# Work lists searched anew, a limit on loads in flight, padded value rows and one last copy in an attention and softplus MLP kernel

## The chip, the core and the metric

The kernel runs on 1 core of one Trainium2 chip. The metric is device microseconds per execution; three executions of the kernel before took 473.81, 474.37 and 475.50 us, so its time is 474.37 us, the median.

## The reference

Four batches of eight heads, 576 positions, head size 64. Attention is taken twice and added: once on means over 4 neighbouring positions (144 by 144 scores, its result repeated 4 times), once on a band of 7 positions around each position. The sum goes, as 2304 tokens by 512, through two weight matrices with a softplus between them.

```python
q_d = q.reshape(B, H, Sd, factor, D).mean(axis=3)      # k_d, v_d likewise, factor 4
out_d = sm_attn(q_d, k_d, v_d)
out_up = np.repeat(out_d, factor, axis=2)
mask = np.abs(pos[:, None] - pos[None, :]) < factor
attn = softmax(where(mask, scale * q @ k.T, -1e9))
x = out_up + attn @ v                                  # to 2304 x 512
h = x @ w_in                                           # 512 x 2048
g = np.maximum(h, 0.0) + np.log1p(np.exp(-np.abs(h)))
return g @ w_out                                       # 2048 x 512
```

## The kernel before

The eight heads of a batch are four pairs, so there are 16 pairs, numbered 0 to 15; pairs 0 to 3 are batch 0. A pair loads four things through SyncE's queue (SP): `q` and `k` (128x584 each, 292 KB), `vr` (the value rows that are averaged, 72 partitions of 4 KB, 288 KB) and `vw` (the windows of values for the band, 384 KB). VectorE reduces q and k to sums of four (`qd`, `kd`, line 487), `block` lays qd out per head (line 456), TensorE makes the pooled scores (`psd`, line 519) and the banded scores (`psc`, line 580). Then come maximum (`mxd`, `mx`), subtraction (`sub`, line 613), exponential, sum, reciprocal and product, transposes (`sT` on VectorE, `pt0` and `pt1` on TensorE with the copies `sdT0` and `sdT1`), the products with the values (`po`, lines 703 and 726), and `x` (line 757), the pair's 128 columns of the MLP's input. The pooled value rows `vd` are made on GpSimd (lines 504, 507).

`xh` and `xl` split x into two parts that add up to it, and each of the 32 weight tiles (512 KB; `iload`, `oload` with the steps `itop`, `ior`, `ihi`, `ilo`) is unpacked and split the same way, so each product of the MLP is three matmuls. The tokens are cut into groups of 512 (five, the last of 256); for each of 16 hidden tiles the first layer is 12 matmuls (line 896, `l1`), the softplus runs on ScalarE, VectorE and GpSimd, and the second layer is 12 matmuls (line 962, `l2`) that run two tiles behind. In group 0 the first layer's tiles 0 to 2 are cut into 4 pieces, one for each pair: `l1_2.0` is the piece of pair 2 in tile 0.

A planner in Python, `Plan.order`, sets the order in which the instructions are written, engine by engine, and so the order of each engine's queue. It keeps a clock of its own from the costs that stand beside each operation. For the first part of the program it doesn't choose: the lists `ORDER` (line 91) say for each engine which operation comes next (`psd.3` is psd of pair 3, `+4` is four filler matmuls on TensorE, line 1052). Where a list ends, the planner takes the ready operation of the lowest priority number.

Listed loads are spaced by two rules. A load is written when the planner's DMA clock is at most `PACE` ahead (line 302), and it gets a wait on the last load that the planner thinks has landed by then (line 321):

```python
o.behind = next((x for x in reversed(loads) if x.end <= t), None)
```

The second layer's results are copied out of PSUM in four chunks of 128 rows for each group; the last chunk of the last group is copied in halves by VectorE and ScalarE, and each half has its own DMA (line 990).

Of the kernel before, what the change touches and what calls it, by code (L numbers as in the profile page):

```python
# [39 lines left out]
HD = SD // 2  # L40
NR = 3
# [56 lines left out]
        qd.0 kd.0 mx.0 sub.0 qd.2 sum.0 sm.0 kd.1 qd.1 mx.2 kd.2 sT.0 ior.0 mxd.0 mx.1 sub.2 mxd.1
        smd.0 qd.3 sub.1 qd.4 oor.0 smd.1 mxd.2 mask.4 sum.2 ior.1 sm.2 sum.1 kd.4 kd.3 sm.1 smd.2
        mx.4 mx.3 sT.1 sub.3 mxd.3 sdT1.1 ior.2 sub.4 sdT0.1 smd.3 od.0 mxd.4 sum.3 x.0 sm.3 sT.2  # L100
        sdT0.2 sdT1.2 x.1 sT.3 ior.3 oor.1 sdT1.3 od.2 smd.4 x.2 ior.4 xl.1 od.3 x.3 ilo.3 xl.3
# [4 lines left out]
        block.0 exp.0 block.1 expd.0 expd.1 exp.1 normd.0 exp.2 itop.1 block.3 ohi.0 sdT0.0 ihi.1
        expd.2 sdT1.0 normd.2 itop.2 exp.3 block.4 ihi.0 expd.3 normd.3 expd.4 xh.0 od.1 itop.3
        otop.1 sdT0.3 ihi.2 xh.1 itop.4 normd.4 xh.2 ihi.3 ihi.4 exp.4 xh.3 ohi.1 itop.5 fill_xh.0
        abs.0 expln.0 abs.2 expln.2 ihi.5 itop.6 abs.1 expln.1 otop.2 ihi.6 sdT1.4 itop.7 abs.3
# [3 lines left out]
        vd.1 norm.0 itop.0 block.2 vd.0 otop.0 normd.1 olo.0 ilo.1 norm.1 vd.2 norm.2 ilo.0 vd.3
        norm.3 xl.0 ilo.2 xl.2 olo.1 ilo.4 gh.0 ilo.5 gh.2 gh.1 otop.3 olo.3
    """,
    "SP": """
        q.0 k.0 q.2 vr.1 q.1 k.2 k.1 iload.0 vr.0 k.4 q.3 q.4 oload.0 iload.1 k.3 iload.2 vw.0 vr.2
        oload.1 vw.1 vr.3 iload.3 vw.2 iload.4 vw.3 k.5 iload.5 iload.6 q.5 vw.4 oload.2 iload.7
# [983 lines left out]
```

## Time and profile before

| | |
|---|---|
| three executions, median | 474.37 us (473.81 to 475.50) |
| profiled execution, its own time | 476.92 us |
| its span, first to last instruction | 475.0 us |
| mean granted TensorE clock | 0.989 |
| TensorE (PE) busy | 460.2 us, 97% |
| VectorE, ScalarE, GpSimd busy | 278.9, 257.0, 99.1 us |
| DMA moved | 42.87 MB, mean 90 GB/s |

The profile is of one execution. The profiled execution's own time is 1.92 us above its span, which is what lies before the first and after the last instruction. A row of the timeline gives start, duration, engine, source line and shapes, and in brackets how long the engine had been idle and who released it; "issue" is a wait for nothing that the profile shows. A record's end on TensorE is modelled, and records of one engine overlap a little, so distances between starts say more than durations. Two records of TensorE (a weight load and a matmul) stand for each step, and an f32 step is done in two passes.

### The profile page before, as it was taken

To read this page: it belongs to the slowest core of one execution; us is meant where nothing else is said; L and a number is where in the kernel's file an instruction comes from. 1 tells how busy PE (TensorE), PEld (TensorE's weight loads), DVE (VectorE), ACT (ScalarE), POOL (GpSimd) and SP (SyncE) were. 2 spreads that over 40 slices of the span, in tenths; PEclk is the share of its full clock that TensorE was granted. 3 is DMA by queue.
4 is the path that set the end of the run, shared out by engine and by line. 5 is a ranking of instruction groups with operands and counts; after the bars stand their busy time and mean duration, and the time that the engine had idled before them with its cause. 6 is when DMAs were issued, how large, how long until landed. Compare 5 with 4: busy or idle time off the path is not lost.

```text
span 475.0 us, 12565 instructions
## 1 busy us (share of the span) xinstructions
PE 460.2 (97%) x5338; PEld 399.2 (84%) x5338; DVE 278.9 (59%) x556; ACT 257.0 (54%) x560; POOL 99.1 (21%) x147
## 2 busy tenths in 40 slices
PE   5799999999999999999999999999999999999996
PEld 3577888888878888888888888888888888889996
DVE  5877888988899666666276647463332222223322
...
GB/s 234 292 227 140 222 158 259 168 210 164 265 100 95 156 2 111 1 110 11 50 52 148 52 61 52 35 1 1 2 88 2 0 2 0 0 1 90 0 1 46
DMA packets 15944, 42.87 MB, mean 90 GB/s; under 512 B 1809, under 2 KB 2449, under 8 KB 15889
## 3 DMA queue, kind: packets, MB, share of 16 engines
...
q8 instruction: 42, 0.69, 0.6%
q14 instruction: 14, 0.11, 0.1%
q10 hardware_dynamic: 144, 0.07, 0.0%
...
## 4 chain that ended last, share of the span: by engine, by line
PE 85%; DMA 6%; DVE 5%; issue 2%; ACT 1%; POOLq 0%; SPq 0%; DVEq 0%; ACTq 0%
PE acc L962 36%; PE h L896 36%; PE psc L580 3%; PE po L726 2%; PE psd L519 2%; PE po L703 2%; PE po L714 2%; DMA qT<-in_qt_dram 2%; DMA kT<-in_kt_dram 2%; PE pdt L678 1%; DMA stage<-in_vrow_dram 1%; DMA wro<-in_w_out_dram 1%; DVE t L926 1%; DVE gl L943 1%; DVE qd L487 1%
## 5 line engine op out<-in xcount | busy, mean ns | idle before, releaser
L935 POOL TENSOR_SCALAR gh<-t 128x512 fp32r<-128x512 f32 (+1 forms) x80 | 53.6, 670 | 292.2 <-DVE t L926 210.1
L917 ACT ACTIVATE t<-h 128x512 f32<-128x512 f32 (+1 forms) x80 | 44.2, 552 | 126.6 <-PE h L896 119.4
L926 DVE SCALAR_TENSOR_TENSOR t<-h,t 128x512 f32<-128x512 f32 (+1 forms) x80 | 50.8, 635 | 92.4 <-ACT t L921 74.7
L943 DVE TENSOR_TENSOR gl<-t,gh 128x512 fp32r<-128x512 f32 (+1 forms) x80 | 52.1, 651 | 42.4 <-POOL gh L935 42.2
L896 PE MATMUL h<-xh,wi0h 128*128 128x512 f32 (+1 forms) x160 | 58.8, 367 | 0.6 <-DVE t L926 0.6
L962 PE MATMUL acc<-gh,wo0h 128*128 128x512 f32 (+1 forms) x160 | 58.3, 364 | 0.0
L896 PE MATMUL h<-xh,wi1h 128*128 128x512 f32 (+1 forms) x160 | 58.0, 362 | 0.2 <-DVE t L926 0.2
L962 PE MATMUL acc<-gh,wo1h 128*128 128x512 f32 (+1 forms) x160 | 57.9, 362 | 0.0
L896 PE MATMUL h<-xl,wi1h 128*128 128x512 f32 (+1 forms) x160 | 57.3, 358 | 0.2 <-issue 0.2
L962 PE MATMUL acc<-gl,wo1h 128*128 128x512 f32 (+1 forms) x160 | 57.4, 359 | 0.1
L896 PE MATMUL h<-xl,wi0h 128*128 128x512 f32 (+1 forms) x160 | 57.3, 358 | 0.0
L896 PE MATMUL h<-xh,wi0l 128*128 128x512 f32 (+1 forms) x160 | 57.3, 358 | 0.0
L962 PE MATMUL acc<-gl,wo0h 128*128 128x512 f32 (+1 forms) x160 | 57.3, 358 | 0.0
L962 PE MATMUL acc<-gh,wo0l 128*128 128x512 f32 (+1 forms) x160 | 57.3, 358 | 0.0
L896 PE MATMUL h<-xh,wi1l 128*128 128x512 f32 (+1 forms) x160 | 57.3, 358 | 0.0
L962 PE MATMUL acc<-gh,wo1l 128*128 128x512 f32 (+1 forms) x160 | 57.3, 358 | 0.0
L920 ACT ACTIVATE t<-t 128x512 f32<-128x512 f32 (+1 forms) x80 | 47.1, 589 | 2.3
L921 ACT ACTIVATE t<-t 128x512 f32<-128x512 f32 (+1 forms) x80 | 47.0, 587 | 2.5
L896 PEld LDWEIGHTS h<-xh,wi0h 128*128 128x128 f32 x160 | 30.3, 189 | 4.4 <-DVE t L926 0.8
L896 PEld LDWEIGHTS h<-xh,wi1h 128*128 128x128 f32 x160 | 30.3, 190 | 4.0 <-DVE t L926 0.6
L896 PEld LDWEIGHTS h<-xh,wi1l 128*128 128x128 f32 x160 | 30.3, 190 | 3.8 <-issue 0.4
L962 PEld LDWEIGHTS acc<-gl,wo1h 128*128 128x128 f32 x160 | 30.3, 190 | 3.5 <-DVE gl L943 0.3
(100 smaller groups left out, 781.3 us busy)
## 6 DMA issues: line engine op xcount, KB each, us to landing
...
```

Of the source, the lines that this page charges most:

```text
L519: nc.tensor.matmul(pd3()[:, r, :], qb[:, r * RD : (r + 1) * RD], kd.t, start=True, stop=True)
L580: nc.tensor.matmul(pc()[o : o + HW, t, :], q.t[hp, c : c + HW], k.t[hp, c : c + HW], start=not early or t == 0, stop=not early, skip_group ...
L703: nc.tensor.matmul(pd()[j * D : (j + 1) * D, :], v[:, c, j, :], sdT.t[:, c, j, :], start=(c == 0 and i == 0), stop=(c == 1 and i == len(vs ...
L714: nc.tensor.matmul(po[i].t[o : o + HW, k * QT : (k + 1) * QT].rearrange("p (h w) -> p h w", h=2), vw.t[kp, t, m * HW : (m + 1) * HW], wide ...
L896: nc.tensor.matmul(turned(h.t, n), w[:, cc, fs], turns(x.t[:, cc], g), start=(cc == 0 and k == 0), stop=(cc == NCC - 1 and k == 2),)
L917: op("ACT", c, pr, lambda: nc.scalar.activation(out=tv(), in_=hh(), func=AF.Abs), r=[h], w=[tt], name=("abs", i))
L920: nc.scalar.activation(out=tv(), in_=tv(), func=AF.Exp, scale=-1.0)
L921: nc.scalar.activation(out=tv(), in_=tv(), func=AF.Ln, bias=1.0)
L926: lambda: nc.vector.scalar_tensor_tensor(out=tv(), in0=hh(), scalar=0.0, in1=tv(), op0=ALU.max, op1=ALU.add),
L935: lambda: nc.gpsimd.tensor_scalar(out=gh.t[:, :, cols(g)], in0=tv(), scalar1=1.0, scalar2=0.0, op0=ALU.mult, op1=ALU.add),
L943: lambda: eng[ge].tensor_tensor(out=gl.t[:, :, cols(g)], in0=tv(), in1=gh.t[:, :, cols(g)].bitcast(F32), op=ALU.subtract),
L962: nc.tensor.matmul(turned(acc[g][m].t, n), w[:, f % FB, ms], turns(a.t, g), start=(f == 0 and k == 0), stop=(f == NF - 1 and k == 2),)
```

## The change

The lists are new ones. The planner's DMA model now moves data at 0.27 instead of 0.305 KB per ns, and spaces listed loads by size: a load waits for that earlier load behind which at most 1000 KB are under way, and the planner adds 0.6 us to its landing. `vr` has 80 partitions instead of 72 (8 rows of padding that the host adds and nothing reads), in all 16 pairs. The last chunk of the last group is one copy of 256 columns by VectorE and one DMA on ScalarE's queue. Costs of two operations that no listed kernel path uses (`sums`, and `po` with `V_PE`, which is empty) change without effect. Fillers in the lists go from 16 to 19.

```diff
+VROWS = 80
 ORDER = {
     "PE": """
-        psc.0 psd.0 psc.2 +1 psc.1 psd.1 psc.4 psd.2 +2 pt0.0 +4 pt1.0 psc.3 pt1.1 +2 psd.3 po.0
+        psc.1 psc.0 psc.4 psd.0 psd.1 +6 psc.2 +3 pt1.0 psd.2 psc.3 +1 pt0.0 +2 psd.4 +2 po.0 pt1.2
...
     "SP": """
-        q.0 k.0 q.2 vr.1 q.1 k.2 k.1 iload.0 vr.0 k.4 q.3 q.4 oload.0 iload.1 k.3 iload.2 vw.0 vr.2
+        q.1 k.1 q.0 k.0 k.4 vr.0 q.4 iload.0 q.2 iload.1 k.2 oload.0 k.3 q.3 vr.2 iload.2 vw.0 vr.3
...
-    DMA_RATE = 0.305
-    PACE = 2.2
+    DMA_RATE = 0.27
+    PACE_KB = 1000
+    SIGNAL = 0.6
...
+    def ahead(self, loads):
+        kb = 0
+        for x in reversed(loads):
+            kb += x.kb
+            if kb > self.PACE_KB:
+                return x
+        return None
...
-                    if fixed and o.kb and dma_free + self.DMA_LAT - self.PACE > t + 1e-9:
-                        continue
+                    if fixed and o.kb:
+                        o.behind = self.ahead(loads)
+                        if o.behind and o.behind.end + self.SIGNAL > t + 1e-9:
+                            continue
...
-                        o.behind = next((x for x in reversed(loads) if x.end <= t), None)
                         loads.append(o)
...
-        vr = abuf(u, "stage", [HD, 2, 2, FACTOR, D], 4, 3)
-        load(vr, vrow[u], u - 56 if early else s + 4, 288, ("vr", u))
+        vr = abuf(u, "stage", [VROWS, 2, 2, FACTOR, D], 4, 3)
+        load(vr, vrow[u], u - 56 if early else s + 4, 300, ("vr", u))
...
-                for e, q, k in (("DVE", "SP", 0), ("ACT", "ACT", 1)):
-                    o = buf("stage", [P, 2, GN], 4, f"osb{g}_{m}{k}")
-                    cs = slice(k * n // 2, (k + 1) * n // 2)
-                    emit(e, q, m, o, lambda o=o: o.t[:, 0, : n // 2], cs)
+                o = buf("stage", [P, 2, GN], 4, f"osb{g}_{m}")
+                emit("DVE", "ACT", m, o, lambda o=o, m=m: o.t[:, 0, :n], slice(0, n))
                 continue
...
+    vrow = _np.pad(vrow.reshape(NU, HD, -1), ((0, 0), (0, VROWS - HD), (0, 0)))
```

What the new lists move is seen in three places. In the rows, the number right after a name is the pair's (`qT0`, `kT1`; `stage1` is `vr` of pair 1, `wri0` is `iload.0`); the number behind it is a buffer's.

SyncE's queue at the start of the program, before:

```order
L427 DMA qT0_138<-in_qt_dram 128x584
L427 DMA kT0_140<-in_kt_dram 128x584
L427 DMA qT2_142<-in_qt_dram 128x584
L427 DMA stage1_144<-in_vrow_dram 72x1024
L427 DMA qT1_148<-in_qt_dram 128x584
L427 DMA kT2_204<-in_kt_dram 128x584
L427 DMA kT1_210<-in_kt_dram 128x584
L828 DMA wri0_219<-in_w_in_dram 128x2047
L427 DMA stage0_278<-in_vrow_dram 72x1024
```

and now:

```order
L437 DMA qT1_138<-in_qt_dram 128x584
L437 DMA kT1_140<-in_kt_dram 128x584
L437 DMA qT0_142<-in_qt_dram 128x584
L437 DMA kT0_144<-in_kt_dram 128x584
L437 DMA kT4_146<-in_kt_dram 128x584
L437 DMA stage0_200<-in_vrow_dram 80x1024
L437 DMA qT4_206<-in_qt_dram 128x584
L838 DMA wri0_262<-in_w_in_dram 128x2047
L437 DMA qT2_276<-in_qt_dram 128x584
```

Two whole pairs (1 and 0) now come first, with pair 4 behind them; pairs 0, 2 and 1 were mixed before, so that the second pair's k was the sixth load and is now the fourth.

VectorE's queue up to the subtraction of pair 3's banded scores (`sc3<-psc3`; `wro0` is the unpacking of a weight tile), before:

```order
L625 TENSOR_REDUCE smp1_70<-sc1_443 128x12
L487 TENSOR_REDUCE kd4_547<-kT4_285 128x144
L487 TENSOR_REDUCE kd3_556<-kT3_434 128x144
L546 TENSOR_REDUCE sm1_559<-smp1_70 128x12
L547 RECIPROCAL sm1_559<-sm1_559 128x12
L546 TENSOR_REDUCE smd2_566<-smdp0_69 96x3
L547 RECIPROCAL smd2_566<-smd2_566 96x3
L608 TENSOR_REDUCE mx4_575<-sc4_476 128x12
L608 TENSOR_REDUCE mx3_584<-psc3_497 128x12
L665 STREAM_TRANSPOSE sT1_589<-sc1_443 128x384
L613 TENSOR_TENSOR sc3_648<-psc3_497,mx3_584 128x384
```

and now:

```order
L618 TENSOR_REDUCE mx2_469<-psc2_384 128x12
L497 TENSOR_REDUCE qd3_477<-qT3_436 128x144
L675 STREAM_TRANSPOSE sT0_490<-sc0_280 128x384
L623 TENSOR_TENSOR sc2_545<-psc2_384,mx2_469 128x384
L540 TENSOR_REDUCE mxd2_549<-psd2_479 96x3
L635 TENSOR_REDUCE smp0_68<-sc2_545 128x12
L618 TENSOR_REDUCE mx3_568<-psc3_492 128x12
L623 TENSOR_TENSOR sc3_573<-psc3_492,mx3_568 128x384
L556 TENSOR_REDUCE sm2_575<-smp0_68 128x12
L557 RECIPROCAL sm2_575<-sm2_575 128x12
L556 TENSOR_REDUCE smd2_583<-smdp0_69 96x3
```

The same work stands ahead of that subtraction except `sm.2`, `smd.2` (two short rows each) and the unpacking `oor.0` (`wro0`), which now stand behind it; it is the 34th listed operation and was the 37th.

The end of ScalarE's queue, before:

```order
L921 ACTIVATE t4_15_5834<-t4_15_5834 128x2x128
L979 COPY osb4_0_5867<-acc4_0_5393 128x256
L979 COPY osb4_2_5870<-acc4_2_5401 128x256
L979 COPY osb4_31_5876<-acc4_3_5405 128x128
L985 DMA out_0_dram<-osb4_31_5876 128x128
```

and now:

```order
L930 ACTIVATE t4_15_5840<-t4_15_5840 128x2x128
L931 ACTIVATE t4_15_5840<-t4_15_5840 128x2x128
L989 COPY osb4_0_5873<-acc4_0_5399 128x256
L989 COPY osb4_2_5876<-acc4_2_5407 128x256
L995 DMA out_0_dram<-osb4_3_5878 128x256
```

ScalarE's half copy of the last chunk is gone, and the DMA that it issues carries the whole chunk.

## Rows read from the trace of the kernel before

**Rows 1.** The page: TensorE's records, and the DMA queue that fetches TensorE's instructions.
```profile
PE 460.2 (97%) x5338; PEld 399.2 (84%) x5338; DVE 278.9 (59%) x556; ACT 257.0 (54%) x560; POOL 99.1 (21%) x147
...
q8 instruction: 42, 0.69, 0.6%
```

**Rows 2.** Windows: busy us and records of five engines, granted clock, DMA share, GB/s.
```profile
24.86:28.27 3.41, 3.17 (x13) 2.45 (x15) 2.44 (x8) 2.61 (x8) 3.33 (x5) 0.50 0.60 190
...
39.49:58.38 18.89, 18.89 (x198) 16.34 (x199) 14.43 (x27) 16.09 (x29) 8.35 (x8) 1.00 0.53 180
58.38:150.00 91.62, 90.61 (x1174) 77.70 (x1173) 80.65 (x146) 71.63 (x151) 22.12 (x22) 1.00 0.55 179
150.00:469.88 319.88, 319.80 (x3102) 282.60 (x3100) 153.81 (x314) 146.02 (x312) 41.84 (x71) 1.00 0.12 40
```

**Rows 3.** Timeline of TensorE, 0 to 60 us.
```profile
9.81 1.01 PE L580 MATMUL psc<-kT,qT 64*32 64x32 f32 x96 [3.33 <-DMA kT<-in_kt_dram]
...
13.66 1.38 PE L580 MATMUL psc<-kT,qT 64*32 64x32 f32 x82 [1.98 <-issue]
...
25.56 1.06 PE L1052 MATMUL busy<-identb 128*128 128x512 bf16 x2
...
27.99 0.83 PE L703 MATMUL po<-sdT,vd 72*64 72x144 f32 x8
...
31.29 1.24 PE L1052 MATMUL busy<-identb 128*128 128x512 bf16 x5
...
39.49 0.43 PE L726 MATMUL po<-sT,vw 32*64 32x24 f32 x16 [0.96 <-issue]
...
58.38 0.38 PE L962 MATMUL acc<-gh,wo0h 128*128 128x512 f32 x1
```

**Rows 4.** Timeline of VectorE, 0 to 45 us.
```profile
3.65 0.75 DVE L487 TENSOR_REDUCE qd<-qT 128x144 f32<-128x576 f32 x1 [2.08 <-DMA qT<-in_qt_dram]
4.35 0.75 DVE L487 TENSOR_REDUCE kd<-kT 128x144 f32<-128x576 f32 x1
...
10.45 0.75 DVE L487 TENSOR_REDUCE kd<-kT 128x144 f32<-128x576 f32 x1 [1.83 <-DMA kT<-in_kt_dram]
...
15.51 0.56 DVE L608 TENSOR_REDUCE mx<-psc 128x12 f32<-128x384 f32 x1 [0.80 <-PE psc L589]
...
19.51 0.68 DVE L850 SCALAR_TENSOR_TENSOR wro<-wro,top 128x512 int32<-128x512 int32 x1
...
22.60 0.23 DVE L547 RECIPROCAL sm<-sm 128x12 f32<-128x12 f32 x1
...
26.82 0.56 DVE L613 TENSOR_TENSOR sc<-psc,mx 128x384 f32<-128x384 f32 x1
```

**Rows 5.** Windows of 10 us, columns as in rows 2.
```profile
0.00:10.00 10.00, 4.95 (x132) 2.73 (x136) 4.89 (x11) 2.45 (x4) 5.90 (x28) 1.00 0.75 218
10.00:20.00 10.00, 7.82 (x305) 6.28 (x293) 8.30 (x16) 4.00 (x17) 5.78 (x8) 0.66 0.93 297
```

**Rows 6.** Timeline of GpSimd, 0 to 45 us.
```profile
8.54 1.26 POOL L504 TENSOR_TENSOR stage<-stage 72x512 f32<-72x512 f32 x1 [2.64 <-DMA stage<-in_vrow_dram]
9.88 0.72 POOL L507 TENSOR_TENSOR vd<-stage 72x256 f32<-72x256 f32 x1
...
13.36 1.02 POOL L458 TENSOR_SCALAR block<-qd 64x144 f32<-64x144 f32 x2
```

**Rows 7.** The chain that ended last, 78 to 88 us.
```profile
78.17 3.65 DMA qT<-in_qt_dram
...
84.32 3.24 DMA stage<-in_vrow_dram
```

**Rows 8.** Timeline of TensorE, 76 to 150 us.
```profile
89.38 0.48 PE L896 MATMUL h<-xh,wi1h 128*128 128x512 f32 x1 [0.16 <-DVE t L926]
```

**Rows 9.** Timeline of all engines, 469.5 to 475 us.
```profile
470.75 0.42 DVE L981 COPY osb<-acc 128x256 f32<-128x256 f32 x1 [0.92 <-PE acc L962]
...
471.74 0.27 ACT L979 COPY osb<-acc 128x128 f32<-128x128 f32 x1 [0.29 <-DVE osb L981]
```

More of the change, by code (lines that the diff above doesn't have):

```diff
@@ L96 @@
+        l1_1.1 l1_2.0 l1_1.2 l1_3.0 l1_2.1 l1_3.1 l1_2.2 pt0.4 l1_3.2 l1_0.3 l1_0.4 l2.0 l2.1
     """,
     "DVE": """
[L98 to L101, printed above, removed]
@@ L102 @@
-        sum.4 ior.5 max.0 sm.4 fill_xl.0 gl.0 max.2 ior.6 max.1 gl.2 qd.5 gl.1 ilo.6 oor.2 norm.4
-        max.3 oor.3 olo.2 sT.4 kd.5 oor.4
+        kd.1 qd.1 qd.0 mx.1 sub.1 kd.4 sum.1 mx.0 sm.1 kd.0 sub.0 qd.4 sum.0 ior.0 qd.2 mask.4 mxd.0
+        mx.4 mxd.1 sT.1 sm.0 smd.0 ior.1 kd.2 smd.1 kd.3 mx.2 qd.3 sT.0 sub.2 mxd.2 sum.2 mx.3 sub.3
+        sm.2 smd.2 ior.2 mxd.4 sub.4 sum.3 oor.0 norm.2 x.0 sT.2 mxd.3 sm.3 norm.3 xl.0 smd.4 sT.3
+        od.2 smd.3 x.2 ior.3 vd.3 od.1 x.1 oor.1 xl.1 sum.4 x.3 ior.4 xl.3 ilo.4 olo.1 ior.5 sm.4
@@ L104 @@
+        max.0 oor.2 max.1 gl.0 ilo.5 norm.4 olo.2 max.2 gl.1 sdT0.4 ior.6 fill_xl.0 oor.3 max.3
+        oor.4
     """,
     "ACT": """
[L106 to L109, printed above, removed]
@@ L110 @@
-        expln.3 abs.4 ohi.2 expln.4 ohi.3 otop.4 sdT0.4 block.5
+        exp.1 exp.0 itop.0 block.1 ihi.0 itop.1 expd.0 expd.1 ihi.1 normd.0 otop.0 sdT1.0 normd.1
+        exp.2 block.4 expd.2 exp.3 sdT0.0 block.3 normd.2 expd.4 od.0 sdT1.2 ohi.0 exp.4 sdT0.2 xh.0
+        ihi.2 itop.3 expd.3 sdT1.1 sdT0.1 normd.3 normd.4 xh.2 sdT1.3 sdT0.3 otop.1 xh.1 sdT1.4
+        ihi.3 od.3 itop.4 xh.3 ohi.1 ihi.4 itop.5 abs.0 expln.0 abs.1 expln.1 ihi.5 ohi.2 abs.2
+        expln.2 otop.3 itop.6 fill_xh.0 abs.3 expln.3 otop.4 itop.7 ohi.3
@@ L111 @@
     """,
     "POOL": """
[L113 to L114 removed]
+        vd.0 block.0 norm.1 block.2 ilo.0 ilo.1 norm.0 vd.2 itop.2 vd.1 ilo.2 olo.0 xl.2 ilo.3
+        otop.2 gh.0 gh.1
     """,
     "SP": """
[L117 to L118 removed]
@@ L342, in order @@
             nxt += [port] if port > t else []
-            nxt += [x.end for x in loads if x.end > t]
-            nxt += [dma_free + self.DMA_LAT - self.PACE] if dma_free + self.DMA_LAT - self.PACE > t else []
+            nxt += [x.end + self.SIGNAL for x in loads if x.end + self.SIGNAL > t]
             for pend in waiting.values():
@@ L504, in pool_v @@
             e.tensor_tensor(
-                out=vr.t[:, :, :, 0:2], in0=vr.t[:, :, :, 0:2], in1=vr.t[:, :, :, 2:4], op=ALU.add
+                out=vr.t[:HD, :, :, 0:2], in0=vr.t[:HD, :, :, 0:2], in1=vr.t[:HD, :, :, 2:4], op=ALU.add
             )
-            e.tensor_tensor(out=vd.t, in0=vr.t[:, :, :, 0], in1=vr.t[:, :, :, 1], op=ALU.add)
+            e.tensor_tensor(out=vd.t, in0=vr.t[:HD, :, :, 0], in1=vr.t[:HD, :, :, 1], op=ALU.add)
         if not v_pe:
@@ L698, in mm_pv @@
         def mm_pv():
-            vs = [vr.t[:, :, :, f] for f in range(FACTOR)] if v_pe else [vd.t]
+            vs = [vr.t[:HD, :, :, f] for f in range(FACTOR)] if v_pe else [vd.t]
             for c in range(2):
@@ L732, in mm_pv @@
                         )
-        op("PE", 1.85 if pair else 2.2, sV + 0.5, mm_pv, r=[vr if v_pe else vd, (sdT, 0), (sdT, 1), vw] + (wide_keys if pair else [sT]), w=po, lat=gap, block=not early, name="po")
+        op("PE", 1.85 if pair else 4.5 if v_pe else 2.2, sV + 0.5, mm_pv, r=[vr if v_pe else vd, (sdT, 0), (sdT, 1), vw] + (wide_keys if pair else [sT]), w=po, lat=gap, block=not early, name="po")
         od = abuf(u, "od", [P, SD], 1, 2)
```

10 lines of the change are left out of this document (5 added, 5 removed).

## The prediction

> **What bounds the kernel now.** I read the windows first, cut where TensorE changes its work. From 58.38 us, where the second layer's second tile begins, to 150 us TensorE is busy 90.61 of 91.62 us, and from there to 469.88 us 319.80 of 319.88 [rows 2]. Behind 58.38 us there is thus 1.1 us to gain, and what the change can move lies ahead of it or in the last 5 us. The timeline of TensorE splits what lies ahead [rows 3]. From 27.99 us, the first `po`, to 58.38 us it goes on without a wait but one, 0.96 us in the middle of a `po`, that is put down to "issue". Ahead of 27.99 us it waits for loads (3.33 us at 9.81), for nothing visible (1.98 us at 13.66), and in one stretch it runs at a granted clock of 0.50, the 1.2 GHz level [rows 2]: two fillers take 1.06 us there, and five take 1.24 us at 2.4 GHz [rows 3]. So two numbers make the time: when the first `po` starts, and what TensorE executes from there to the common point M, at which batch 0's four `po`, pair 4's transposes, five tiles of the first layer and one of the second are done (58.38 us).
>
> **When the first po starts.** In the new list, `psd.4` and two fillers stand ahead of `po.0`. `psd.4` takes one of the two PSUM banks, which comes free when VectorE has subtracted pair 3's banded scores (`sub.3`). So VectorE's queue sets this start. That subtraction ended at 26.82 + 0.56 = 27.38 us [rows 4], 23.7 us after VectorE's first reduction at 3.65. In those it waited 1.83 us for the k that was the sixth load and 0.80 us for scores that TensorE's stall held back; other waits were under 0.7 us. The new list takes three entries out of the way: `oor.0`, 0.68 us, and `sm.2` and `smd.2`, four short rows that I price at 0.23 each [rows 4], together 1.6 us. The work itself is then 23.7 - 1.83 - 0.80 - 1.6 = 19.5 us. It now begins with `kd.1` and so at the second load, which VectorE got at 4.35 us or earlier [rows 4]; that gives 23.85 us with no wait of these two kinds. Do they come back? The order of loads gives VectorE two whole pairs at once, and the waits on pair 2's mix are gone. What is late next is k of pair 4, the fifth load, and q of pair 4, the seventh; I add 0.4 us for them: 24.3 us. Two fillers and a `psd` took from 25.56 to 27.99, 2.4 us, at the lower clock [rows 3], so about 1.2 at the higher: `po.0` starts between 25.5 and 26.7 us. From below it is bounded by its own load: `vw.0` is the 17th load in both lists with 6.1 MB up to its end; 5.15 MB had moved by 20 us, and at 297 GB/s [rows 5] the rest takes 3.2 us, at the mean of 258 GB/s 3.7, after which it still has to land: 24 to 25 us. From above: if the waits of 1.83 and 0.80 us come back, it is 28.0 us, as before. I take 26.0 us, nearer the lower end, because VectorE's own work leads there, and keep 25.0 and 28.0.
>
> Off this path on TensorE: `psc.4` is now the third `psc`, as `psc.1` was when TensorE stalled for 1.98 us [rows 3]; nothing needs its scores before `mask.4`, the 16th entry of VectorE's list, so a stall there costs nothing up to some 3 us. Were that cover gone, the stall would go to `psd.0` and on to VectorE. On GpSimd `block.0` now stands behind `vd.0`, and so behind the sixth load. That load was served at 9.81 us [rows 3]; 1.26 + 0.72 + 1.02 us [rows 6] put `psd.0` at 12.8 us. `mxd.0` is the 17th entry of VectorE's list, some 10 us behind 4.35, so 1.5 us are left; with a stage load that lands 2 us late VectorE would stand for 0.5 us. I count nothing.
>
> **From po.0 to M.** 58.38 - 27.99 = 30.39 us, less the issue wait of 0.96, is 29.4 us [rows 3]. The new list has five fillers there instead of seven, -0.5 us at 0.25 each, and three transposes more, which I price between nothing and those fillers, 0.4 us: 29.3 us. The issue wait may come again or not; I count half, 0.5 us. M is then at 26.0 + 29.3 + 0.5 = 55.8 us: 2.6 us earlier, with 25.0 + 29.3 = 54.3 (-4.1) and 28.0 + 30.3 = 58.3 (-0.1) as ends. The Trainium skill, "Runtime: NRT & Kernel Launch", section "Instruction fetch mechanics", says that instructions come in blocks of 256 by a DMA of the engine's own and that this is mostly hidden. Rows agree with the size, 42 packets of 0.69 MB for 10,676 records, 254 each [rows 1]; not with the hiding, if the waits of 1.98 and 0.96 us are fetches. By that rule the half wait falls away and the sum would be 0.5 us better.
>
> **Behind M.** TensorE's work is the same; 1.1 us of waits remain as they are. A start 2.6 us earlier meets softplus and weights on VectorE and ScalarE earlier. At 89.38 us TensorE already waits 0.16 us for VectorE [rows 8], so there is no reserve in that spot. But the chain that leads there starts at TensorE itself: q of pair 6 is loaded when TensorE has freed its buffer at 78.17 us [rows 7], so most of it moves along. I add 0.3 us, between 0 and 2.6.
>
> **The padding.** 16 loads carry 32 KB more, four of them early: 0.13 MB, at most 0.4 us of DMA time at 297 GB/s [rows 5], inside the 24 to 25 us above. A lone 72-row load took 3.24 us, a q load next to it 3.65 [rows 7]; nothing there shows that 72 rows are slow. The Trainium skill, "DMA: Bandwidth & Descriptors", section "Why a DMA increments its semaphore by 16 and not by 1", has a load run on the largest number of engines up to 16 that divides its rows: 12 for 72, 16 for 80, so five rows for each engine instead of six. By it a lone load would be up to 0.5 us shorter (estimate, a sixth of 3.24); the sum stays, since no `vr` ends last on the path above.
>
> **The end.** ScalarE's half copy waited 0.29 us for VectorE's half and ended at 472.01 us. VectorE now copies 256 columns from the same start, 471.45, in 0.42 us [rows 9], so the last DMA goes out at 471.9 us instead of 472.0, and SyncE has one issue less. It carries 128 KB instead of 64. -0.2 us, between -0.4 and +0.2.
>
> **Sum.** -2.6 + 0.3 - 0.2 = -2.5 us. The profiled execution took 476.92 us, 2.55 above the median; 474.4 there is 471.9 us as a run.
>
> **Rivals.**
> 1. *The other engines hold the second layer.* If VectorE and ScalarE don't come forward with TensorE, what was gained at M is waited for between 58 and 110 us. For it: no reserve at 89.38 us [rows 8]. Against: VectorE is busy 80.65 of 91.62 us [rows 2], and the chain starts at TensorE. Time: 474.4 - 0.2 = 474.2 us, no change.
> 2. *The start isn't earlier.* The new rule lets 1000 KB be under way, but the queue was mostly full before: DMA share 0.93 in 10 to 20 us [rows 5]. If loads set `po.0` and land as before, only the end and the padding remain: 474.2 us. Against: the first `po` wasn't held by its load but by TensorE's and VectorE's queues.
> 3. *Instructions come late.* More loads under way share the DMA engines with the fetch of TensorE's instructions. A `po` uses some 208 records in 2.3 us; one of the four stalled 0.96 us, and a denser stretch earlier 1.98 [rows 3]. If all four stall by 1.5 us, the mean of those two, M comes 6.0 - 0.5 = 5.5 us later than forecast: 477.4 us, slower. It is slower by over 0.3% from 1.1 us per `po` on. Against: the share was near its limit already. The same page of the Trainium skill speaks against it, since it has the fetch hidden.
>
> **How the numbers follow.** Of this kernel 0.3%, 1.4 us, can be told from no change. Forecast: 0.60, with a range of its own of 470.1 to 473.6; 0.56 of it is faster by over 1.4 us, 0.04 not. Rival 1: 0.15, of which 0.04 slower (waits that exceed what was gained). Rival 2: 0.11, of which 0.02 slower. Rival 3: 0.14, of which 0.12 slower. Together faster 0.56, same 0.26, slower 0.18. The range runs from 469.9 (both lower ends of the sum, -4.1 and -0.4) to 475.3, which takes in rivals 1 and 2 and leaves out most of rival 3.
>
> **What would show it.** Right: `po.0` at 25 to 27 us, `sub.3` ending ahead of 25 us, the second tile of the second layer at 54.5 to 57 us, no new wait of TensorE over 1 us between there and 110 us, the last output DMA going out 0.1 us after the copy. Wrong: a first `po` at 28 us or later (rival 2); waits of TensorE for VectorE or ScalarE that grow behind 58 us (rival 1); issue waits within the `po` groups that sum to over 4 us (rival 3).

## The result, and the profile after

The changed kernel takes **481.42 us** (median of 4 executions, 480.44 to 481.92), the kernel before 474.94 (473.81 to 475.54, 4). The ratio is 1.0137 with a 95% interval of 1.0109 to 1.0165: slower by 1.4%, where 471.9 us was forecast. The profiled execution took 481.25 us with a span of 479.5, against 476.92 and 475.0 of before. By the profiles it is thus 4.3 us slower, by the medians 6.5, since the profiled execution of before lay 2 us above its median.

TensorE first: its timeline, with the first `po`, the first tile of the first layer (`l1_0.0`), the third `po`, and the common point M.

```profile
25.85 0.71 PE L713 MATMUL po<-sdT,vd 72*64 72x144 f32 x8
26.49 1.59 PE L736 MATMUL po<-sT,vw 32*64 32x24 f32 x96
...
33.41 0.57 PE L906 MATMUL h<-xh,wi0h 128*128 128x512 f32 x1
35.31 0.80 PE L906 MATMUL h<-xl,wi0h 128*128 128x512 f32 x1 [1.33 <-DVE xl L789]
...
36.46 1.23 PE L713 MATMUL po<-sdT,vd 72*64 72x144 f32 x8
37.62 2.88 PE L736 MATMUL po<-sT,vw 32*64 32x24 f32 x96
...
64.05 0.38 PE L972 MATMUL acc<-gh,wo0h 128*128 128x512 f32 x1
```

The first `po` starts at 25.85 us instead of 27.99 [rows 3], as forecast. M comes at 64.05 instead of 58.38. What lies between has grown from 30.39 to 38.20 us. Two things in these rows do it: a wait of 1.33 us for VectorE's `xl`, and `po` groups that take 1.23 and 2.88 us where the first `po` took 0.71 and 1.59. The windows, the first two cut where the granted clock changes, show the second (columns as in [rows 2]):

```profile
17.32:34.38 17.06, 15.19 (x455) 11.11 (x453) 15.71 (x34) 15.08 (x51) 9.14 (x9) 1.00 0.83 261
34.38:51.45 17.07, 16.14 (x232) 13.10 (x233) 10.52 (x24) 8.78 (x19) 3.78 (x4) 0.50 0.50 163
...
58.38:150.00 91.62, 91.53 (x1180) 78.99 (x1179) 83.14 (x148) 73.81 (x151) 15.57 (x20) 1.00 0.57 184
...
150.00:469.88 319.88, 319.88 (x3085) 282.32 (x3084) 155.47 (x318) 148.21 (x317) 42.23 (x70) 1.00 0.13 41
```

For 17 us TensorE runs at the 1.2 GHz level although it is busy for 16.14 of them. The clock fell 0.4 us after the wait for `xl` had begun, so 0.93 us of the wait lie in that stretch. Before, TensorE had 3.4 us at that level around the start of the first `po`, and from there to M none [rows 2]. Behind 58.38 us TensorE waits 0.09 us instead of 1.1.

Why `xl` was late stands in the timelines of VectorE and GpSimd:

```profile
23.84 0.56 DVE L623 TENSOR_TENSOR sc<-psc,mx 128x384 f32<-128x384 f32 x1
...
31.58 3.67 DVE L789 TENSOR_TENSOR xl<-x,xh 128x512 fp32r<-128x512 f32 x1
```
```profile
29.92 1.28 POOL L514 TENSOR_TENSOR stage<-stage 72x512 f32<-72x512 f32 x1 [4.14 <-DMA stage<-in_vrow_dram]
31.27 0.97 POOL L517 TENSOR_TENSOR vd<-stage 72x256 f32<-72x256 f32 x1
32.21 1.26 POOL L885 TENSOR_TENSOR wi0l<-wri,wi0h 128x512 fp32r<-128x512 f32 x1
33.44 1.27 POOL L885 TENSOR_TENSOR wo0l<-wro,wo0h 128x512 fp32r<-128x512 f32 x1
```

`xl.0` took 3.67 us. The same subtraction takes 0.68 us on VectorE elsewhere in this trace. It started inside a row of GpSimd operations (`vd.1`, `ilo.2`, `olo.0`) that follow one another with no gap, and it ended at 35.25 us, 0.54 behind the row's last. The row began when `vr.1` had landed, 4.14 us after GpSimd had become free. The new list loads `vr.1` as the 20th of its loads (before, as the fourth), and puts `xl.0` on VectorE (before, on GpSimd).

The chain of waits runs through it (start, duration, what):

```profile
31.66 3.60 DVE xl L789
35.26 0.04 issue
35.31 1.22 PE h L906 x2
```

The end, a timeline of all engines:

```profile
475.92 0.42 DVE L991 COPY osb<-acc 128x256 f32<-128x256 f32 x1 [0.24 <-PE acc L972]
476.38 0.37 ACTq L995 DMA_DIRECT2D out_dram<-osb  x1
```

The DMA goes out 0.04 us after VectorE's copy has ended, and the span ends 3.1 us behind that; before, the DMA went out at 472.03 us and the span ended 2.9 behind.

### The profile page after: what moved, and what is told of

Same layout as the page of the kernel before. It is cut to its first block, busy times and chain, and to the rows that moved or that the text cites. A ratio compares the mean times of both kernels' runs of the same rounds, so it can differ in the third digit from the quotient of the medians.

```text
span 479.5 us, 12567 instructions
## 1 busy us (share of the span) xinstructions
PE 467.8 (98%) x5341; PEld 405.3 (85%) x5341; DVE 283.3 (59%) x559; ACT 259.5 (54%) x566; POOL 82.7 (17%) x139
## 4 chain that ended last, share of the span: by engine, by line
PE 92%; DMA 5%; DVE 2%; POOL 1%; issue 0%; POOLq 0%; SPq 0%
PE h L906 40%; PE acc L972 39%; PE po L736 2%; PE psc L590 2%; PE po L713 2%; DMA stage<-in_vrow_dram 2%; PE po L724 2%; PE psd L529 2%; PE pdt L688 2%; DMA wro<-in_w_out_dram 1%; DMA qT<-in_qt_dram 1%; DVE xl L789 1%; DMA kT<-in_kt_dram 1%; POOL stage L514 0%; DVE sc L642 0%; DVE mxd L540 0%
## 5 line engine op out<-in xcount | busy, mean ns | idle before, releaser
L945 POOL TENSOR_SCALAR gh<-t 128x512 fp32r<-128x512 f32 (+1 forms) x80 | 49.2, 615 | 303.0 <-DVE t L936 209.0
L953 DVE TENSOR_TENSOR gl<-t,gh 128x512 fp32r<-128x512 f32 (+1 forms) x80 | 51.3, 641 | 41.6 <-POOL gh L945 41.4
L906 PE MATMUL h<-xh,wi0h 128*128 128x512 f32 (+1 forms) x160 | 60.3, 377 | 0.0
L906 PE MATMUL h<-xl,wi0h 128*128 128x512 f32 (+1 forms) x160 | 58.8, 367 | 1.3 <-DVE xl L789 1.3
L906 PE MATMUL h<-xh,wi0l 128*128 128x512 f32 (+1 forms) x160 | 58.6, 366 | 0.0
L906 PEld LDWEIGHTS h<-xl,wi0h 128*128 128x128 f32 x160 | 31.1, 195 | 5.0 <-DVE xl L789 1.7
L906 PEld LDWEIGHTS h<-xh,wi0l 128*128 128x128 f32 x160 | 31.1, 194 | 3.6
L972 PEld LDWEIGHTS acc<-gh,wo0h 128*128 128x128 f32 x160 | 30.3, 189 | 3.6
```

The source lines that it names most:

```text
L906: nc.tensor.matmul(turned(h.t, n), w[:, cc, fs], turns(x.t[:, cc], g), start=(cc == 0 and k == 0), stop=(cc == NCC - 1 and k == 2),)
L945: lambda: nc.gpsimd.tensor_scalar(out=gh.t[:, :, cols(g)], in0=tv(), scalar1=1.0, scalar2=0.0, op0=ALU.mult, op1=ALU.add),
L953: lambda: eng[ge].tensor_tensor(out=gl.t[:, :, cols(g)], in0=tv(), in1=gh.t[:, :, cols(g)].bitcast(F32), op=ALU.subtract),
L972: nc.tensor.matmul(turned(acc[g][m].t, n), w[:, f % FB, ms], turns(a.t, g), start=(f == 0 and k == 0), stop=(f == NF - 1 and k == 2),)
```

## The experiments

Theory T: GpSimd's row holds up `xl.0`, TensorE stands idle for it, and the clock falls. Its rivals: A, `xl.0` is slow for another reason; B, the clock falls whatever that wait does; C, pacing, padding or the last chunk lose the time; and, from the first runs on, F, the forecast's third rival: instructions come late. Each ratio is to the kernel before in the same comparison. In these comparisons single executions of one edited kernel spread by 0.4 to 2%, those of the kernel before by 2 to 3%, so a ratio's interval is about 0.003 to 0.005 wide on either side. A profile is one draw: those of e2, e6, e8 and e14 are of the slowest execution of their kernel. "Mean clock" is the granted clock, averaged over a kernel's executions.

**First comparison: one piece at a time**

`e1_olo_later`, one entry of GpSimd's list:
```diff
-vd.1 ilo.2 olo.0 xl.2 ilo.3
+vd.1 ilo.2 xl.2 olo.0 ilo.3
```


> The changed kernel with one entry of GpSimd's list moved: olo.0 behind xl.2, so that GpSimd's last operation beside VectorE's xl.0 is ilo.2. Theory T (VectorE's subtraction xl.0 took 3.67 instead of 0.69 us because GpSimd worked back to back beside it; TensorE's wait of 1.33 us that followed brought the 1.2 GHz stretch of 17 us): GpSimd's row ends at about 33.5 instead of 34.7, xl.0 ends near 34.0 instead of 35.25, TensorE's wait is under 0.4 us; if the clock then holds the time is 473 (half clock of 17 us gone, some 6.5 us, and 1.2 us of wait), if it still falls 480. Rival A (xl.0 is slow for a reason that isn't GpSimd, loads for one): xl.0 still takes over 3 us and the time is 481. Rival B (the clock falls whatever this wait does, for what TensorE did earlier): xl.0 is shorter and the half clock comes all the same, 480.

Measured: 1.0085 (1.0050 to 1.0120), mean clock 0.980. The gain didn't come. The timelines of VectorE and GpSimd say why: `vr.1` landed later still, so the shorter row ran at the same time.

```profile
34.22 2.43 DVE L789 TENSOR_TENSOR xl<-x,xh 128x512 fp32r<-128x512 f32 x1
```
```profile
33.96 0.92 POOL L517 TENSOR_TENSOR vd<-stage 72x256 f32<-72x256 f32 x1
34.85 1.26 POOL L885 TENSOR_TENSOR wi0l<-wri,wi0h 128x512 fp32r<-128x512 f32 x1
```
GpSimd's row ends at 36.11 us, `xl.0` at 36.65, again 0.54 behind it. TensorE waited 1.92 us and 13.65 us of half clock followed. So one entry less is no cure while the load is late; the mechanism is the same, which speaks against A.

`e2_fillers`, in TensorE's list:
```diff
-pt0.1 +1 l1_0.0
+pt0.1 +9 l1_0.0
```


> The changed kernel with nine fillers instead of one ahead of the first tile of the first layer, l1_0.0, so that TensorE executes about 8 x 0.215 = 1.7 us of filler matmuls where it otherwise waits. Theory T: xl.0 still takes over 3 us, but TensorE has no idle stretch over 0.7 us between 30 and 36 us, its granted clock stays at 2.4 GHz, and the time is 475 (some 6.5 us better than the changed kernel, 0.3 lost on fillers). Rival B: the half clock comes all the same, 481. Rival A says the same as T here, as it disputes only why xl.0 is slow.

Measured: 0.9991 (0.9954 to 1.0028), mean clock 0.991: the loss is gone within the interval. But in its profile `xl.0` came a moment ahead of GpSimd's operation and took 0.68 us, so the profile doesn't show a filled wait. It shows other stalls: 2.37 us for issue in the middle of `psc.3` and 0.92 us in `po.3`, each with 3.4 us of half clock. The fillers also give late instructions time, 0.22 us for each, so this run alone doesn't tell T from F.

`e3_vr1_early`, in SyncE's list (with e1's edit):
```diff
-vw.0 vr.3 vw.2 vr.1 iload.3
+vw.0 vr.1 vr.3 vw.2 iload.3
```


> The changed kernel with the load of pair 1's value rows, vr.1, ahead of vr.3 and vw.2 instead of behind them, and olo.0 behind xl.2 on GpSimd. Theory T: vr.1 lands two loads (some 2 us) earlier, GpSimd does vd.1 by 29 us instead of 31 and ilo.2 ahead of xl.0; xl.0 takes under 2 us, TensorE waits under 0.4 us for it, the clock stays at 2.4 GHz from 18 us on, M (the second tile of the second layer) is at 55.5 to 57.5 us instead of 64.05, and the time is 472.5, below the kernel before. Rival A: xl.0 still takes over 3 us, 481. Rival B: half clock again, 480.

Measured: 0.9982 (0.9932 to 1.0032); the median of its executions isn't below the kernel before's. `vd.1` was done at 29.77 us. `xl.0` fell beside one GpSimd operation, `ilo.2`, took 1.76 us and ended 0.55 behind it, and nobody waited for it (VectorE, GpSimd):

```profile
34.28 1.76 DVE L789 TENSOR_TENSOR xl<-x,xh 128x512 fp32r<-128x512 f32 x1
```
```profile
34.06 1.43 POOL L885 TENSOR_TENSOR wi0l<-wri,wi0h 128x512 fp32r<-128x512 f32 x1 [4.29 <-ACT wi0h L879]
```
M was at 60.70, not at 55.5 to 57.5, because TensorE waited in its timeline at another place:

```profile
24.22 0.85 PE L590 MATMUL psc<-kT,qT 64*32 64x32 f32 x45 [3.10 <-issue]
```
A part of T holds, and F comes in as a second possible cause.

`e4_old_lists`: the five lists of the kernel before in the changed kernel.
```diff
-(the changed kernel's ORDER)
+(the ORDER of the kernel before)
```


> The changed kernel with the five lists of the kernel before; the pacing rule of 1000 KB, the data rate, the padding and the last chunk's copy stay as changed. Theory T (the whole loss comes of the new lists at one place): 475, within 1 us of the kernel before, with half clock for some 3.4 us from 25 us on as before and none from 35 to 52 us. Rival C (the loss lies in pacing, padding or the last chunk): 479 to 482.

Measured: 1.0013 (0.9974 to 1.0052). Its M is at 58.62 us, as before, with half clock from 38.6 to 42.0 us and none other behind 22 us. Windows, columns as in [rows 2]:

```profile
29.29:38.59 9.30, 9.13 (x271) 7.12 (x272) 7.45 (x19) 7.28 (x23) 9.14 (x9) 1.00 0.86 262
38.59:42.01 3.42, 3.42 (x14) 2.36 (x14) 3.39 (x9) 1.52 (x4) 0.64 (x1) 0.50 0.75 239
```
TensorE had been busy for 9.13 of the 9.30 us ahead of that fall, with no single wait over 0.2 us. So a stretch of half clock can also come without a wait right ahead of it, and what brought this one stays open. Pacing, padding and last chunk with the old lists change nothing that can be told; C falls. The loss comes with the new lists.

**Second comparison: where the wait comes from**

`e5_again` is the changed kernel, with no edit.

> The changed kernel as it is, once more, beside the three that follow and on the same chip: where the data lands at other times, the stall may sit in another place. All theories: ratio to the kernel before 1.010 to 1.016. Theory T, sharpened by the runs so far (VectorE's subtraction of two SBUF tensors, xl.0, waits until GpSimd ends the last of its back-to-back operations, and ends 0.55 us behind it): where xl.0 starts within GpSimd's row of vd.1, ilo.2 and olo.0 it ends 0.50 to 0.60 us behind that row, TensorE waits 1 to 2 us ahead of the first tile of the first layer, and half clock follows within 1.5 us for over 10 us. Rival F (late instructions): what stretches the start is the wait for issue in the middle of psc.3, and half clock follows that one.

Measured: 1.0066 (1.0022 to 1.0111), mean clock 0.978. That is slower again, but by 3 us and not the 6.5 of the first result, and below the 1.010 that was expected. The collision is there again, the same (timelines of VectorE, GpSimd, TensorE):

```profile
32.55 3.68 DVE L789 TENSOR_TENSOR xl<-x,xh 128x512 fp32r<-128x512 f32 x1
```
```profile
34.41 1.27 POOL L885 TENSOR_TENSOR wo0l<-wro,wo0h 128x512 fp32r<-128x512 f32 x1
```
```profile
36.28 0.48 PE L906 MATMUL h<-xl,wi0h 128*128 128x512 f32 x1 [1.33 <-DVE smd L556]
```
The row ends at 35.68, `xl.0` at 36.23: 0.55 behind. (TensorE's wait is put down to the `smd` that VectorE did next; the operand it lacked is `xl`.) Half clock ran from 38.9 to 49.2 us here, 2.7 us behind the wait and not within 1.5 as expected. This profile has no wait for issue behind 18 us. Its first `po` started at 27.28 us, behind a wait of 1.19 us for a q.

`e6_xl0_gpsimd`:
```diff
 DVE:  -norm.3 xl.0 smd.4              +norm.3 smd.4
 POOL: -vd.1 ilo.2 olo.0 xl.2          +vd.1 xl.0 ilo.2 olo.0 xl.2
```


> The changed kernel with xl.0 taken from VectorE's list and put on GpSimd, directly behind vd.1 and ahead of ilo.2 and olo.0. Theory T: nothing is left to collide, xl.0 takes 1.3 us and ends 1.3 us behind vd.1, some 1.7 us ahead of where it ended on VectorE; TensorE's wait ahead of the first layer is under 0.5 us; no half clock between 32 and 50 us; ratio to the kernel before 0.993 to 1.000, 12 to 17 thousandths below the changed kernel. Rival F: half clock stays behind the psc.3 wait or the po, ratio as of the changed kernel.

Measured: 1.0026 (0.9983 to 1.0069), mean clock 0.984. Nothing collides any more, but `vd.1` waits for its load and `xl.0` waits for `vd.1`:

```profile
33.37 1.29 POOL L789 TENSOR_TENSOR xl<-x,xh 128x512 fp32r<-128x512 f32 x1
```
```profile
34.71 0.72 PE L906 MATMUL h<-xl,wi0h 128*128 128x512 f32 x1 [1.49 <-POOL xl L789]
```
From the start of `vd.1` to the end of `xl.0` it takes 3.3 us here and 5.3 to 5.4 in the two profiles of the changed kernel: the collision costs 2 us there. The late load alone still leaves 1.49 us, and 17 us of half clock follow in this profile, which is of the slowest of the ten executions. The expectation (wait under 0.5 us, no half clock, ratio at most 1.000) missed on that.

`e7_pace600`:
```diff
-PACE_KB = 1000
+PACE_KB = 600
```


> The changed kernel with 600 instead of 1000 KB of loads under way. Rival F (instructions of TensorE queue behind data: the wait for issue in the middle of psc.3 was 0.46 to 3.10 us in four profiles): fewer data ahead of the fetch, the wait in psc.3 is under 0.5 us and the ratio falls by 5 thousandths or more below the changed kernel's. Theory T: loads come later still, vr.1 lands at 30.5 us or later, xl.0 collides with GpSimd again, ratio 1.010 to 1.020.

Measured: 1.0100 (1.0059 to 1.0141). No wait for issue over 0.2 us from 18 to 60 us, as F said, but the ratio didn't fall below the changed kernel's. Loads come later: `vr.1` let GpSimd start only at 35.20 us, and TensorE waited 2.53 us for pair 1's transposed scores ahead of its `po`. `xl.0` was through ahead of the row and did not collide, against T's expectation. Half clock followed this other wait too, from 40.5 to 54.1 us.

`e8_both` puts e3's load order, e6's place of `xl.0` and four more fillers together:
```diff
 SP:   -vw.0 vr.3 vw.2 vr.1 iload.3    +vw.0 vr.1 vr.3 vw.2 iload.3
 DVE:  -norm.3 xl.0 smd.4              +norm.3 smd.4
 POOL: -vd.1 ilo.2 olo.0 xl.2          +vd.1 xl.0 ilo.2 olo.0 xl.2
 PE:   -pt0.1 +1 l1_0.0                +pt0.1 +5 l1_0.0
```


> The changed kernel with vr.1 loaded ahead of vr.3 and vw.2, xl.0 on GpSimd directly behind vd.1, and five fillers instead of one ahead of the first tile of the first layer. Theory T: vd.1 ends by 30 us, xl.0 is off VectorE, TensorE waits under 0.3 us there, no half clock from 30 to 43 us; ratio to the kernel before 0.990 to 0.997, the best of all. Rival F: psc.3 waits 2 us or more for issue all the same and eats the gain, 0.997 to 1.003.

Measured: 0.9938 (0.9894 to 0.9983), mean clock 0.993, the best in this comparison. No wait ahead of the first layer and full clock from 16 to 43 us, though `vd.1` ended at 31.8 us and not by 30; then 2.32 us for issue in `po.3`, with 6.8 us of half clock.

**Third comparison: does the idle time bring the clock down, and what does F cost**

`e10_idle` and `e11_filled` start from e8_both and plant a late `xl.0` that has nothing to do with VectorE; they differ in the fillers alone:
```diff
 POOL: -vd.1 xl.0 ilo.2 olo.0 xl.2     +vd.1 ilo.2 olo.0 xl.0 xl.2
 PE:   -pt0.1 +5 l1_0.0                +pt0.1 +1 l1_0.0      (e10_idle)
 PE:   -pt0.1 +5 l1_0.0                +pt0.1 +12 l1_0.0     (e11_filled)
```


> The kernel of e8_both (vr.1 earlier, xl.0 on GpSimd) with xl.0 put behind ilo.2 and olo.0 on GpSimd and one filler ahead of the first layer: a wait is planted that has nothing to do with VectorE. Theory T, second step (an idle TensorE there brings the 1.2 GHz stretch): xl.0 ends 2.5 us later than in e8_both, TensorE waits 1.5 to 2.5 us for GpSimd ahead of its first tile of the first layer, half clock of 10 us or more follows within 4 us, time 5 to 8 us over e8_both's, ratio to the kernel before 1.004 to 1.012. Rival B (the clock falls for another reason): half clock doesn't follow the wait, the time is that of e8_both plus the wait, ratio 0.997 to 1.000.

> As e10_idle, with twelve fillers instead of one: the first tile of the first layer starts at about the same time, but TensorE executes 11 x 0.215 = 2.4 us of filler matmuls where it waited. Theory T: no wait over 0.5 us and no half clock from 33 to 43 us, ratio 0.995 to 1.001, 5 us or more ahead of e10_idle though each tile starts no earlier. Rival B: same time and clock as e10_idle.

Measured: e10_idle 1.0081 (1.0048 to 1.0113), mean clock 0.979; e11_filled 1.0001 (0.9964 to 1.0038), mean clock 0.993. TensorE's timeline and the windows, e10_idle first:

```profile
34.67 0.80 PE L906 MATMUL h<-xl,wi0h 128*128 128x512 f32 x1 [1.87 <-POOL xl L789]
```
```profile
34.22:51.29 17.07, 16.62 (x233) 13.43 (x234) 8.73 (x16) 8.15 (x18) 4.16 (x4) 0.50 0.39 130
```
```profile
32.47 2.76 PE L1060 MATMUL busy<-identb 128*128 128x512 bf16 x12
34.87 0.57 PE L906 MATMUL h<-xh,wi0h 128*128 128x512 f32 x1
35.28 0.38 PE L906 MATMUL h<-xl,wi0h 128*128 128x512 f32 x1
```
```profile
34.22:51.29 17.07, 16.08 (x261) 13.04 (x259) 10.26 (x21) 10.70 (x23) 4.70 (x4) 0.90 0.64 215
```
The matmul with `xl.0` starts at 34.67 us in the one and at 35.28 in the other. Idle ahead of it, TensorE ran 17 us at half clock, from 0.45 us before the wait's end on; filled, none until a wait for issue of 0.99 us in `po.3` brought 3.4 us. M came at 63.60 and 59.28, the spans are 479.6 and 474.4 us. This is the cleanest pair of the study: TensorE had its operand at nearly the same time in both, yet the idle 1.87 us cost 5 us by the spans and by the medians (481.71 and 476.48), 4 by the ratios. B falls for this place.

`e12_pace800` and `e9_pace1400` are e8_both with another amount of loads under way:
```diff
-PACE_KB = 1000
+PACE_KB = 800      (e12_pace800)
+PACE_KB = 1400     (e9_pace1400)
```


> The kernel of e8_both with 800 instead of 1000 KB of loads under way. Rival F as a second cause (TensorE's instructions queue behind data; e8_both still waited 0.60 us in psc.3 and 2.32 us in po.3 for issue): the issue waits from 20 to 46 us sum to under 1.5 us, ratio to the kernel before 0.988 to 0.996. Without F: loads land some 0.5 to 1 us later and the ratio is 0.995 to 1.002.

> The kernel of e8_both with 1400 instead of 1000 KB of loads under way. Rival F: more data ahead of each fetch, the issue waits from 20 to 46 us sum to over 4 us, ratio 1.000 to 1.010. Without F: loads land earlier or as they did, ratio 0.990 to 0.997.

Measured: 1.0071 (1.0038 to 1.0104) with 800 KB, 1.0036 (1.0005 to 1.0066) with 1400. TensorE's timeline of the one, then of the other:

```profile
11.22 1.59 PE L590 MATMUL psc<-kT,qT 64*32 64x32 f32 x96 [3.33 <-DMA qT<-in_qt_dram]
```
```profile
12.74 1.28 PE L590 MATMUL psc<-kT,qT 64*32 64x32 f32 x75 [1.43 <-issue]
...
25.36 0.85 PE L590 MATMUL psc<-kT,qT 64*32 64x32 f32 x45 [2.71 <-issue]
```
With 800 KB there is no wait for issue at all, and the loads are waited for instead (3.33 us here, 1.25 at the next q, 1.68 for a `vw`). With 1400 KB the waits for issue sum to 4.9 us from 10 to 47 us, of which 3.4 lie behind 20 (not the over 4 that I expected there). F's direction is seen at the lower end: no wait for issue from 9 to 66 us in the profiles with 600 and 800 KB, and at least one in each profile with 1000. At the upper end it isn't shown, since in three profiles of e8_both's kernel with 1000 KB the waits behind 20 us sum to 2.9, 1.0 and 3.7. Both ends are slower than e8_both's kernel; with 800 KB the limit trades one wait for the other. My ratios for 800 KB missed, as they left out the loads.

**Fourth comparison: xl.0 ahead of vd.1, and a repeat**

`e13_xl0_first` and `e14_first_early`:
```diff
 DVE:  -norm.3 xl.0 smd.4              +norm.3 smd.4
 POOL: -itop.2 vd.1 ilo.2              +itop.2 xl.0 vd.1 ilo.2
 SP:   -vw.0 vr.3 vw.2 vr.1 iload.3    +vw.0 vr.1 vr.3 vw.2 iload.3   (e14 only)
 PE:   -pt0.1 +1 l1_0.0                +pt0.1 +5 l1_0.0               (e14 only)
```


> The changed kernel with xl.0 on GpSimd ahead of vd.1 (e6_xl0_gpsimd had it behind); loads, fillers and all else as changed. Theory T1 (the wait came from vr.1's landing, by way of GpSimd's row): xl.0 ends at 33 us, 1.3 us after x.0 is there; TensorE's wait ahead of the first tile of the first layer is under 0.4 us, vd.1 is done at 35 us and po.1 waits for it at most 0.8 us; ratio to the kernel before 0.995 to 1.002. Theory T2 (the collision alone is the loss, vr.1's lateness isn't): ratio as of e6_xl0_gpsimd or better, 0.993 to 1.003, but by the same token no wait in either, which e6's 1.49 us already speaks against. Rival: po.1 now waits over 1.2 us for vd.1, half clock comes from there, ratio 1.003 to 1.010.

> As e13_xl0_first, with vr.1 loaded ahead of vr.3 and vw.2 and five fillers instead of one. Theory T1: neither xl.0 nor vd.1 is waited for over 0.4 us, no half clock from 28 to 42 us but behind waits for issue; ratio 0.989 to 0.997, like e8_both. Rival: the gain of e8_both was chance, 0.997 to 1.003.

`e15_both_again` has no edit against e8_both.

> The kernel of e8_both again (0.9938, 0.9894 to 0.9983). Theory T1: 0.990 to 0.998 again, TensorE's wait ahead of the first layer under 0.5 us. Rival (that one was chance): 0.998 to 1.004.

Measured: e13_xl0_first 1.0063 (1.0028 to 1.0099), e14_first_early 1.0004 (0.9968 to 1.0040), e15_both_again 0.9987 (0.9947 to 1.0026). In e13 the wait ahead of the first layer is gone, as T1 has it, and `po.1` doesn't wait for `vd.1`. TensorE went at full clock into `po.1` and ran out of instructions there:

```profile
39.12 0.64 PE L736 MATMUL po<-sT,vw 32*64 32x24 f32 x18 [1.87 <-issue]
```
10 us of half clock followed. So taking the one stall away uncovered the other, and the time is that of the changed kernel: T1's ratio missed. In e14 the five fillers and the early load bring it back to the kernel before, not below; its profile has 1.74 us for issue in `po.3`, with 6.8 us of half clock. e15 repeats the profile of e8_both (no wait ahead of the first layer) but not its gain: two comparisons give 0.9938 and 0.9987.

**Fifth comparison: the break in po.3**

`e16_po3_later`, from e8_both:
```diff
-l1_0.1 pt1.4 po.3 l1_0.2 l1_1.0 l1_1.1 l1_2.0 l1_1.2
+l1_0.1 l1_0.2 l1_1.0 l1_1.1 l1_2.0 pt1.4 po.3 l1_1.2
```


> The kernel of e8_both with pair 3's transposes and value product, pt1.4 and po.3, put behind four more tiles of the first layer (l1_0.2, l1_1.0, l1_1.1, l1_2.0), so that twelve slow 512-column matmuls stand ahead of the record at which TensorE waited for issue, and that record falls behind po.3. Rival F as the second cause (the fetch is asked for at about the same record, some 200 ahead, and queues behind data): no wait for issue over 0.3 us from 34 to 50 us, no half clock from 36 to 55 us, M at 56.5 to 58 us, ratio to the kernel before 0.987 to 0.996, and 2 us or more below e18_both_third. Without F: the wait stays, ratio as of e18_both_third.

> The kernel of e8_both once more, as the comparison for e16_po3_later: ratio to the kernel before 0.993 to 1.000, a wait for issue of 0.5 to 2.5 us in po.3 with half clock of 3 to 7 us behind it, if F holds.

Measured: e16 1.0071 (1.0039 to 1.0103), e18 0.9990 (0.9950 to 1.0029). TensorE's timeline of e18, then of e16:

```profile
44.06 0.35 PE L736 MATMUL po<-sT,vw 32*64 32x24 f32 x10 [2.60 <-issue]
```
```profile
43.00 0.48 PE L906 MATMUL h<-xh,wi0h 128*128 128x512 f32 x1 [0.55 <-ACT xh L466]
...
50.19 0.80 PE L906 MATMUL h<-xh,wi0h 128*128 128x512 f32 x1 [1.13 <-ACT xh L466]
```
Twelve slow matmuls ahead of the break took the wait for issue away, as F has it (0.19 us is left, in `po.1`). But `po.3` now comes later, and pieces of the first layer stand for an `xh` that isn't there yet, with 3.4 us of half clock behind the second of these waits. From the start of the third `po` to M this profile and e18's take the same time within 0.2 us, so the expected gain went into new waits. M is at 63.40 us against 60.79 in e18, but 2.4 of these 2.6 us came ahead of the edited place (e16's first `po` started 1.1 us later, and it waits 0.44 us for a `vw` and 1.31 for pair 2's transposed scores). By the ratio the edit is worse than none; whether it brought those earlier delays isn't shown.

## Why the prediction was wrong

**When the first po starts: right.** `sub.3` ended at 24.40 us (forecast 24.3, "ahead of 25 us") and `po.0` started at 25.85 (forecast 26.0). The two waits of VectorE that were said to go are gone, and `psc.4` in third place did no harm. That it came so close is partly luck: VectorE waited 1.29 us at 13.19 for ScalarE's unpacking of a weight tile, which was not counted, and its other work was shorter than forecast by as much. In e5's profile of the same kernel VectorE waited 1.72 us for a q and `po.0` started at 27.28 us, outside the 25 to 27 of the prediction.

**From po.0 to M: this step failed.** It put the stretch at "30.39 us, less the issue wait of 0.96", with two fillers less, three transposes more and half an issue wait: 29.8 us, M at 55.8. It was 38.20, M at 64.05. The executed work was about what was forecast. What the step left out:
- a wait of 1.33 us for `xl.0` and one of 0.23 for issue, against the 0.5 that was counted: +1.1 us;
- 17.07 us at 1.2 GHz, 16.14 of them busy. Two `po` took 4.11 and 4.00 us instead of the 2.30 of the first one, which is 3.5 us; the other 8.0 us of busy time, mostly 512-column matmuls 0.43 us apart instead of 0.216, are worth half, 4.0: together +7.5 us.

These make 8.6 us, against the 8.4 by which the stretch came out longer than forecast; the rest of it was 0.2 us shorter than the forecast had it. The step took TensorE's own list of before and carried its length over as if it were a constant. It never asked when the operands of `l1_0.0` would be there, although the diff moved `xl.0` to VectorE and `vr.1` from the fourth load to the 20th, and although the trace of before has GpSimd operations of 0.72 and 1.26 us [rows 6] that would now fall beside it. And it had no term for the clock in this stretch: [rows 2] showed 3.4 us at half clock around the start of the first `po`, but I priced only fillers there.

**Behind M: the sign was wrong.** I added 0.3 us. It became 1.2 us shorter: span less M is 415.45 instead of 416.62. TensorE waits 0.09 us there instead of 1.1, and at [rows 8] none. What made it shorter stays open: over all profiles span less M is 415.1 to 417.6 us, with no relation to M (415.12 in e11 with M at 59.28, 416.26 in e1 with M at 64.24, 417.05 in e15 with M at 58.55). Rival 1 was not put to the test, since no profile of the new lists has M ahead of 58.4 us.

**The padding: right so far as it goes.** A load of 80 rows with no other under way when it was issued landed in 3.0 us, the 72-row load in 3.24 [rows 7]. The DMA view of the stretch from 69.5 to 69.7 us:

```profile
stage<-in_vrow_dram SPq DMA_DIRECT2D x1, 320.0 KB, 3.0
```
The forecast's estimate by the Trainium skill, "DMA: Bandwidth & Descriptors", section "Why a DMA increments its semaphore by 16 and not by 1", was up to 0.5 us; here it is 0.2, of one load each, and the next load was issued 1.9 us behind the one and 0.9 behind the other, so the rows alone don't bear the 0.2. e4_old_lists, with the padding, is no faster than before.

**The end.** Forecast -0.2 us, within -0.4 to +0.2. The last DMA goes out 0.04 us behind its copy (0.02 before [rows 9]); the gap from the start of TensorE's last matmul group to the copy's end shrank from 0.91 to 0.73 us, and the larger DMA took 0.1 us longer. In sum 0.0.

**Rival 3** (instructions come late) had the right sign for a reason that the profiled execution did not show: its issue waits in the four `po` sum to 0.23 us. In other executions they are real (3.10 us in `psc.3`, 2.32 and 2.60 in `po.3`). The traces show by the times that they are waits for fetched instructions (their places, in the last section, agree), which answers the prediction's "if" on the 1.98 and 0.96 us of before. Of the 46 waits for issue over 0.2 us between 9 and 66 us in the 19 profiles, 45 end 1.2 to 1.7 us behind the end of a packet on the queue that fetches TensorE's instructions (q8 in [rows 1]); the exception is 0.66 us in the kernel before. In the eight longest, 1.87 to 3.10 us, the packet began less than 0.5 us before or after TensorE had run out. In e18, for one, TensorE ran out at 41.46 us, and the DMA view from 36.5 to 41.6 us has no packet of that queue; from 41.6 to 42.7 us it has:

```profile
q8 instruction: 1, 0.02, 5.5%
```
TensorE went on at 44.06 us. In e15, the same kernel, the packet ahead of that place began at 39.26 us and the wait was 0.59 us. What makes the packet late is not shown in a row. That loads hold it back is argued from the profiles with 600 and 800 KB, and the DMA share alone doesn't say it: from the time when TensorE was at the same earlier record (37.27 us in e15, 37.46 in e18) to the packet it was 0.96 in e15 and 0.77 in e18.

What stays open: how the loss, 6.5 us by the first medians and 3 in e5, shares out between the late `xl.0` and late instructions over all executions. Either can be enough: e6 takes the collision away and falls to half clock by the late load, and e13 takes the wait for `xl.0` away and falls by late instructions. That is why fillers at the place (e2, e11, e8, e14, e15) brought the time back to that of the kernel before, and removal of one cause (e1, e6, e13) did so partly or not at all. No version is shown to beat the kernel before: e8_both was at 0.9938, 0.9987 and 0.9990, whose last two intervals hold 1. It does beat the changed kernel in the comparison that had both.
